# A new hand-written order for the first 36 tiles, with some small steps moved between ScalarE and VectorE

## The chip, the cores and the metric

The kernel runs on one core of a Trainium2 chip. The metric is device time in microseconds, the median of three runs; lower is better.

## The reference

A chunked attention with memory tokens feeds two feed-forward layers, all in fp32. Cut to what matters:

```python
def _attn_ref(q, k, v, mem_k, mem_v):           # 4 x 8 heads, 768 tokens, head size 64
    for c in range(nc):                         # chunks of 32 queries
        k_ctx = k[:, :, l_start:r_end]          # 16 tokens to the left, 8 to the right
        k_full = np.concatenate([mem_k, k_ctx], axis=2)     # 8 memory tokens in front
        scores = scale * np.matmul(q_c, k_full.transpose(0, 1, 3, 2))
        a = np.exp(scores - np.max(scores, axis=-1, keepdims=True))
        a = a / (np.sum(a, axis=-1, keepdims=True) + 1e-09)
        out[:, :, c_start:c_end] = np.matmul(a, v_full)

def _moe_ref(x, w_in, w_out, s, b):             # x 3072 x 512, w_in 512 x 2048
    r = np.maximum(x @ w_in, 0.0)
    return (s * (r * r) + b) @ w_out

def _moe2_ref(x, w_in, w_out):
    h = x @ w_in
    return (h - np.tanh(h)) @ w_out
```

## The kernel before

The 3072 tokens are 24 units of 128 tokens (attention) and 6 blocks of 512 (the layers). A full-precision product is three matmuls on split operands: a rounded upper part and a remainder of both the weights and the data (helper `three`, lines 227 to 229). The order of work of the first 36 up-projection tiles is not found by a scheduler: the string `START` lists it token by token, and each engine runs its own instructions in that order. A token is a step and a number:

- Attention of unit u: `qk` and `vv` load its operands; `S` computes scores on TensorE (line 357); `M` scales and masks them out of PSUM (VectorE, line 380); `R` takes the row maximum (VectorE, line 390); `E` is eight exponentials on ScalarE, each followed by the read-out of its sum (line 398); `D` is a reciprocal and the division (VectorE, lines 412 and 413; a small addition on GpSimd stands before them); `T` transposes on TensorE (line 422 for whole heads, eight instructions, or line 429 for half heads, sixteen); `C` is two copies out of PSUM (ScalarE, line 437); `V` multiplies by the values (TensorE, line 466); `X` and `L` make the upper part (ScalarE, line 484) and the remainder (VectorE, line 488) of the result. Units 0 and 1 come in halves, marked a and b.
- Up-projection weights n = 0 to 7 of the first layer: `ra` loads the words; `z` scales (ScalarE, line 234); `i` shifts (VectorE, line 240); `o` fills (VectorE, line 250); `h` writes the upper part (ScalarE, line 541); `l` the remainder (VectorE, line 545). Tiles 2n and 2n+1 of a block need weights n.
- Tile p: `F` is its 12 products on TensorE (`G` and `F` halves for tiles 0 and 1), into PSUM bank 5 + p mod 3; `r` is the relu (ScalarE, line 572); `Q` the square (ScalarE, line 584, for the tiles in `SCALAR_SQUARES`, else VectorE, line 586). Tile p + 3 can't start before the square of tile p has read that bank.
- `k`, `K`, `st` combine (VectorE, line 598) and store four tiles; `wl`, `ws`, `wf`, `wd`, `wc`, `ww` prepare weights of the second layer (`wc` is four VectorE sums on 128x256, lines 936 and 864; `ww` stores them).

Behind `START` a loop runs tiles 36 to 95, with the same order in both kernels. For tile 36 it says: the products, then the exponentials of unit 16, then the relu of tile 36, then its square:

```python
        up1_products(n)
        ...
            if i8 in (0, 2) and a + i8 // 2 < NU:
                exponentials(a + i8 // 2)
        ...
        up1_relu(n)
        up1_square(n)
```

So on ScalarE the relu of tile 36 stands behind the exponentials of unit 16, and these need `R16`, the last VectorE step of `START`. The tables under `START` (`SCORES_AT`, `TURNS_AT`, `VALUES_BETWEEN`) choose PSUM banks for units; `WHOLE_TURNS` chooses the form of the transposes.

Of the kernel before, what the change touches and what calls it, by code (L numbers as in the profile page):

```python
# [8 lines left out]
F32 = mybir.dt.float32  # L9
# [26 lines left out]


START = """
qka1 Sa1 Ma1 Ra1 Ea1 qkb0 qka0 qkb1 Sb0 Mb0 Rb0 Sa0 Eb0 Ma0 Ra0 Ea0 Sb1 Mb1 Rb1 qk2 Eb1 qk3 S2 M2
qk4 R2 S3 vv0 qk5 S4 vv1 D0 M3 T0 S5 E2 R3 D1 M4 C0 D2 E3 V0 R4 T1 T2 ra0 C1 vv2 X0 D3 M5 V1 T3 vv3  # L40
C2 z0 X1 qk6 L0 i0 C3 h0 V2 L1 V3 S6 o0 l0 G1 ra1 X2 qk7 G0 R5 M6 L2 E4 ra2 vv4 X3 D4 T4 z1 S7 i1
qk9 qk8 L3 h1 E5 o1 F0 l1 z2 r0 C4 F1 R6 i2 F2 h2 E6 Q0 ra3 F3 o2 D5 l2 M7 T5 V4 C5 qk10 D6 r2 R7 S9
z3 r3 S8 i3 ra4 M9 Q2 r1 o3 F5 h3 X4 F4 l3 T6 R9 Q1 z4 E7 L4 M8 vv5 i4 o4 r4 F6 h4 qk11 ra5 Q4 r5 R8
F7 Q5 Q3 z5 l4 C6 r7 F8 S10 vv7 i5 k0 S11 h5 r6 vv9 vv6 V5 o5 E8 Q7 X5 r8 l5 M10 V6 D7 X6 D8 K0 ra6
T7 z6 F11 Q6 E9 F9 qk13 C7 M11 ra7 z7 r9 i6 L6 k1 L5 o6 qk12 h6 R11 F10 i7 h7 D9 T8 S12 r10 l6 C8
st0 vv8 E11 M12 V7 S13 o7 T9 Q8 M13 r11 R13 F12 F13 E13 l7 qk15 X7 R10 Q11 qk14 K1 C9 wl1 F14 S15
vv11 D13 D11 L7 M15 R15 S14 Q9 Q10 ws1 r13 r12 M14 V9 E15 V8 T13 T11 st1 wf1 F15 C11 wc1 qk17 r14
D15 k2 Q12 V11 Q14 S17 r15 X11 L11 wl0 vv13 F18 M17 ww1 F17 R17 E10 Q13 D10 K2 Q15 X9 C13 X8 r17 T10
L9 T15 C10 R14 vv10 V13 L8 V10 k3 C15 r18 K3 F16 r16 R12 F21 X10 st2 E12 F19 Q16 L10 Q18 Q17 r19 r21
F20 F24 Q19 r20 E14 F22 r22 qk16 D12 st3 Q20 F23 r23 Q21 F25 k4 Q22 F26 ws0 Q23 K4 r24 r26 F27 st4  # L50
D14 k5 r25 K5 Q24 F28 Q25 Q26 r27 wd1 F29 st5 Q27 F30 r29 r28 Q29 k6 K6 r30 st6 Q28 F31 F32 X13 Q30
r31 L13 T12 T14 Q31 r32 k7 K7 Q32 F35 r35 F34 Q35 C12 r34 F33 vv12 Q34 wf0 r33 st7 wc0 S16 V12 Q33
k8 K8 wd0 ww0 st8 X12 M16 L12 R16 C14
"""

WEIGHTS2 = {
# [19 lines left out]
for q in (3, 4, 5, 6):  # L76
# [5 lines left out]
PAIRED, UP_FIRST = 16, 36  # L82
QUARTERS = [(j, q) for j in range(2) for q in range(4)]
SCALAR_SQUARES = {
    1, 2, 3, 6, 7, 8, 9, 10, 11, 12, 13, 14, 15, 16, 17, 18, 20, 21, 22, 23, 24, 25, 29, 31, 32, 34,
    35, 39, 47, 89, 90, 91, 92, 93,
}
WHOLE_TURNS = {
    0, 2, 3, 6,
}  # L90
SCORES_AT = {
    0: 5, 1: 2, 2: 0, 3: 5, 4: 0, 5: 5, 6: 0, 7: 2, 8: 0, 9: 2, 10: 0, 11: 2, 12: 0, 13: 2, 14: 0,
    15: 2, 16: 2, 17: 0,
}
TURNS_AT = {
    0: 2, 1: 0, 2: 2, 3: 0, 4: 0, 5: 0, 6: 2, 7: 0, 8: 2, 9: 0, 10: 2, 11: 0, 12: 2, 13: 2, 14: 0,
    15: 0,
}
VALUES_BETWEEN = {
    0, 2, 6, 8, 10, 11,  # L100
}
HIGH_ON_VECTOR = set()
COPY_ON_VECTOR = set()
PLAIN_EXPONENTIALS = set()

P2_STEPS = {}
for m, n, at in ((2, 44, (-2, 1, 2, 6)), (3, 52, (-2, 1, 2, 6)), (4, 60, (-2, 1, 2, 6)), (5, 68, (-2, 1, 2, 6)),
# [34 lines left out]
def tile_chunk_attention_two_ffn(  # L142
# [42 lines left out]
    def new(place, n, dt, name):  # L185
        assert n <= SIZE[place[0]], (place, n)
        if place[0] in "QSRYWV":
            assert place[0] in side["letters"], place
        pool = arena if place[0] in "EZ" else side["of"]
        return pool.tile([P, n], dt, tag=place, name=name)  # L190
# [201 lines left out]
    def exponentials(u, w=None):  # L392
        if u not in sum_t:
            sum_t[u] = small.tile([P, 8], F32, tag="sums", name="sums")
        sm, nmx, sums = sm_t[u], mx_t[u], sum_t[u]
        total = (u, w) not in PLAIN_EXPONENTIALS
        for h in range(8) if w is None else (2 * w, 2 * w + 1, 4 + 2 * w, 5 + 2 * w):
# [1025 lines left out]
```

## Time and profile before

| | |
|---|---|
| median of 3 runs | 1028.63 us (1028.47 to 1029.04) |
| the profiled execution | 1029.12 us, its span 1027.3 us |
| TensorE busy | 1015.4 us, 99% |
| VectorE busy | 788.6 us, 77% |
| ScalarE busy | 573.2 us, 56% |
| granted TensorE clock | 1.00 |

The profile gives start and length of every instruction. Rows of a timeline hold: start and length in us, engine, line, operation, what is written from what, shape, count, and in brackets how long the engine stood idle before and what ended that. Neighbours on an engine overlap a little (one starts before the end of the one in front), so the distance of two starts, not the length, is the price of one in a row. Matmul lengths overlap most: the price of a 128x512 one is the distance of starts.

### The profile page before, as it was taken

How to read it: one execution, taken by the hardware profiler on the slowest of the kernel's cores; microseconds unless marked ns; L12 is line 12 of the kernel's file. 1: busy time of each engine (PE TensorE's matmuls, PEld its weight loads, DVE VectorE, ACT ScalarE, POOL GpSimd, SP SyncE). 2: the span in 40 equal slices, each digit the busy share in tenths (PEclk: the TensorE clock that was granted, in tenths of full speed). 3: DMA queues.
4: the chain of work that ended last, by engine and by line, in shares of the span. 5: the costliest groups of instructions: out<-in, count | busy, mean ns of one | idle time of the engine just before them, and what ended most of it. 6: DMA issues, size and time to landing. Idle time of an engine off the chain costs nothing.

```text
span 1027.3 us, 15607 instructions
## 1 busy us (share of the span) xinstructions
PE 1015.4 (99%) x6112; PEld 842.0 (82%) x6112; DVE 788.6 (77%) x970; ACT 573.2 (56%) x1055; POOL 11.3 (1%) x53
## 2 busy tenths in 40 slices
PE   7999999999999999999999999999999999999998
PEld 5888888888888888888888888888888888888887
DVE  7999446888677878898788788888888966767654
ACT  8999635666435575666555544455445554444432
POOL 1000000000000000000000000000000000000000
PEclk9999999999999999999999999999999999999999
DMA  9798558888889997796652265655569995555761
GB/s 348 295 330 335 243 220 324 327 334 301 325 322 376 387 336 256 259 337 192 209 196 82 113 247 210 238 215 216 226 260 357 364 328 180 200 205 213 256 248 63
DMA packets 78506, 268.94 MB, mean 262 GB/s; under 512 B 5728, under 2 KB 5984, under 8 KB 67168
## 3 DMA queue, kind: packets, MB, share of 16 engines
q1 hardware_dynamic: 78432, 267.94, 70.8%
q8 instruction: 48, 0.79, 0.3%
q14 instruction: 26, 0.21, 0.1%
HBM read 160.96 MB, written 106.95 MB: 261 GB/s over the span
## 4 chain that ended last, share of the span: by engine, by line
PE 93%; DVE 3%; ACT 2%; DMA 1%; issue 0%; SPq 0%; DVEq 0%; ACTq 0%
PE pb L227 30%; PE pb L229 29%; PE pb L228 29%; PE pb L466 2%; PE pb L357 1%; PE pb L429 1%; ACT sm L398 1%; DMA o<-ob 1%; DMA qk<-in_qk_dram 1%; DVE oa L1167 0%; DVE nmx L390 0%; DVE sm L380 0%; DVE oa L864 0%; ACT pt L437 0%; DVE ob L864 0%
## 5 line engine op out<-in xcount | busy, mean ns | idle before, releaser
L228 PE MATMUL pb<-ringhringl,whl 128*128 128x512 f32 (+1 forms) x680 | 262.9, 387 | 0.0
L227 PE MATMUL pb<-ringhringl,whl 128*128 128x512 f32 (+1 forms) x680 | 262.8, 387 | 0.0
L229 PE MATMUL pb<-ringhringl,whl 128*128 128x512 f32 (+1 forms) x680 | 262.8, 386 | 0.0
L738 ACT ACTIVATE ringhringl<-part 128x1024 fp32r<-128x1024 f32 x120 | 127.0, 1060 | 149.0 <-PE pb L229 146.1
L739 DVE TENSOR_TENSOR ringhringl<-part,ringhringl 128x1024 fp32r<-128x1024 f32 x120 | 146.8, 1223 | 73.3 <-ACT ringhringl L738 73.0
L227 PE MATMUL pb<-xh,w 128*128 128x512 f32 (+1 forms) x392 | 152.9, 390 | 0.3 <-DVE oa L586 0.3
L228 PE MATMUL pb<-xh,w 128*128 128x512 f32 (+1 forms) x392 | 151.0, 385 | 0.1
L229 PE MATMUL pb<-xl,w 128*128 128x512 f32 (+1 forms) x392 | 151.0, 385 | 0.0
L229 PEld LDWEIGHTS pb<-ringhringl,whl 128*128 128x128 f32 x680 | 127.7, 188 | 26.1
L228 PEld LDWEIGHTS pb<-ringhringl,whl 128*128 128x128 f32 x680 | 127.7, 188 | 25.9
L227 PEld LDWEIGHTS pb<-ringhringl,whl 128*128 128x128 f32 x680 | 127.7, 188 | 25.7
L572 ACT ACTIVATE r<-pb 128x512 f32<-128x512 f32 x96 | 56.6, 595 | 91.9 <-PE pb L229 90.1
L227 PE MATMUL pb<-x2hx2l,w 128*128 128x512 f32 x224 | 87.3, 390 | 0.2 <-ACT keep L1163 0.2
L227 PEld LDWEIGHTS pb<-xh,w 128*128 128x128 f32 x392 | 73.6, 188 | 16.6 <-DVE oa L586 1.0
L228 PE MATMUL pb<-x2hx2l,w 128*128 128x512 f32 x224 | 87.2, 389 | 0.0
L229 PE MATMUL pb<-x2hx2l,w 128*128 128x512 f32 x224 | 87.1, 389 | 0.0
L229 PEld LDWEIGHTS pb<-xl,w 128*128 128x128 f32 x392 | 73.7, 188 | 15.0
L228 PEld LDWEIGHTS pb<-xh,w 128*128 128x128 f32 x392 | 73.7, 188 | 14.4 <-DVE w L545 0.3
L586 DVE TENSOR_TENSOR oa<-pb,r 128x512 f32<-128x512 f32 x62 | 42.5, 688 | 49.3 <-ACT r L572 49.3
L733 ACT ACTIVATE ringhringl<-part,b_c 128x1024 fp32r<-128x1024 f32 x48 | 55.1, 1151 | 34.1 <-PE pb L229 32.3
L1175 ACT ACTIVATE pb<-oa 128x512 f32<-128x512 f32 x72 | 43.2, 600 | 55.3 <-DVE oa L1167 54.4
L398 ACT ACTIVATE sm<-sm,nmx 128x96 f32<-128x96 f32 x192 | 69.2, 369 | 3.5 <-DVE nmx L390 3.5
(131 smaller groups left out, 1382.0 us busy)
## 6 DMA issues: line engine op xcount, KB each, us to landing
part<-o SPq DMA_DIRECT2D x84, 512.0 KB, 4.9
part<-o SPq DMA_DIRECT2D x42, 1024.0 KB, 6.2
o<-ob SPq DMA_DIRECT2D x24, 1024.0 KB, 5.4
o<-oa SPq DMA_DIRECT2D x24, 1024.0 KB, 3.9
o<-oa SPq DMA_DIRECT2D x24, 768.0 KB, 5.4
o<-ob SPq DMA_DIRECT2D x24, 768.0 KB, 5.1
raw<-in_wi_dram SPq DMA_DIRECT2D x16, 1024.0 KB, 6.4
raw<-in_wo_dram SPq DMA_DIRECT2D x16, 1024.0 KB, 8.2
```

The source lines that it names most:

```text
L227: nc.tensor.matmul(acc, lhsT=whi, rhs=xhi, start=first, stop=False, skip_group_check=more)
L228: nc.tensor.matmul(acc, lhsT=wlo, rhs=xhi, start=False, stop=False, skip_group_check=more)
L229: nc.tensor.matmul(acc, lhsT=whi, rhs=xlo, start=False, stop=last, skip_group_check=more)
L357: nc.tensor.matmul(score_bank(u, g)[QE * e:QE * (e + 1), KE * (r0 + r):KE * (r0 + r + 1)], lhsT=tq[sl, r, QE * e:QE * (e + 1)], rhs=tk[sl, ...
L398: nc.scalar.activation(out=sm[:, h, :], in_=sm[:, h, :], func=AF.Exp, bias=nmx[:, h:h + 1], scale=1.0, **({"accum_out": sums[:, h:h + 1]} ...
L466: nc.tensor.matmul(value_bank(u)[64 * g:64 * g + 64, c0:c0 + QE], lhsT=tv[0:KE, e, 2 * r + g, :], rhs=pt[0:KE, e, 4 * g + r, :], start=Tru ...
L572: nc.scalar.activation(out=r, in_=up_ps[p], func=AF.Relu)
L586: nc.vector.tensor_tensor(out=o, in0=ps2, in1=r2, op=ALU.mult)
L733: nc.scalar.activation(out=xh, in_=src, func=AF.Identity, bias=self.bias)
L738: nc.scalar.activation(out=xh, in_=src, func=AF.Copy)
L739: nc.vector.tensor_tensor(out=xl, in0=src, in1=xh.bitcast(F32), op=ALU.subtract)
L1175: nc.scalar.activation(out=self.rs[o], in_=src, func=AF.Tanh)
```

## The change

`START` is a new list of the same tokens, plus `Ua1`, `U10` and `U14`. Where these stand, the exponentials of that unit (the first half of unit 1; units 10 and 14) run without the read-out of sums, and one VectorE reduction makes the sums. The upper part of weights 1, 2, 3, 4 and 6 is written by VectorE in place of ScalarE, as a multiplication by a per-partition scalar. The two copies of units 12 and 14 go to VectorE. `SCALAR_SQUARES` gains tiles 0, 4, 5, 19, 27, 28, 30 and 33, and loses 20, 22 and 23: 27 of the first 36 squares stood on ScalarE, now 32. Three units are transposed whole (0, 3, 8), before four (0, 2, 3, 6). The bank tables differ too. The code for all of this was there before; its tables were empty.

```diff
-k8 K8 wd0 ww0 st8 X12 M16 L12 R16 C14
...
+k6 r31 K6 Q31 L13 r32 k7 st6 wd0 Q32 K7 F35 F33 F34 r35 C12 ww1 Q35 qk16 r33 Q33 vv12 V12 r34 Q34 k8
+K8 X12 wc0 L12 st7 C14 ww0 S16 M16 R16 st8
 """
...
 WHOLE_TURNS = {
-    0, 2, 3, 6,
+    0, 3, 8,
 }
...
-HIGH_ON_VECTOR = set()
-COPY_ON_VECTOR = set()
-PLAIN_EXPONENTIALS = set()
+HIGH_ON_VECTOR = {
+    1, 2, 3, 4, 6,
+}
+COPY_ON_VECTOR = {
+    12, 14,
+}
+PLAIN_EXPONENTIALS = {
+    (1, 0), (10, None), (14, None),
+}
```

VectorE at the end of the list, before: the last combine (`k8`, `K8`), then `M16`, `L12`, `R16`; behind them stand the squares of tiles 36 and 37.

```order
L586 TENSOR_TENSOR oa<-pb,r 128x2x256
L598 TENSOR_TENSOR ob<-oa 128x512
L598 TENSOR_TENSOR ob<-oa,ob 128x512
L598 TENSOR_TENSOR ob<-oa 128x512
L598 TENSOR_TENSOR ob<-ob,oa 128x512
L380 SCALAR_TENSOR_TENSOR sm<-pb,mask_mid 128x768
L488 TENSOR_TENSOR xl<-pb,xh 128x4x128
L390 TENSOR_REDUCE nmx<-sm 128x8
L586 TENSOR_TENSOR oa<-pb,r 128x2x256 x2
```

The same place now (the lines stand six further down in the file):

```order
L604 TENSOR_TENSOR ob<-ob,oa 128x512
L942 TENSOR_TENSOR raw<-zw 128x256
L870 TENSOR_TENSOR raw<-zw 128x256
L870 TENSOR_TENSOR raw<-raw,zw 128x256
L870 TENSOR_TENSOR raw<-zw,raw 128x256
L494 TENSOR_TENSOR xl<-pb,xh 128x4x128
L441 COPY pt<-pb 96x512 x2
L386 SCALAR_TENSOR_TENSOR sm<-pb,mask_mid 128x768
L396 TENSOR_REDUCE nmx<-sm 128x8
L592 TENSOR_TENSOR oa<-pb,r 128x2x256 x2
```

The four sums of `wc0` and the two copies of `C14` now stand between the last combine and the maximum of unit 16.

ScalarE at the same place, before: the copies of unit 14, the eight exponentials of unit 16, the relus of tiles 36 and 37.

```order
L484 ACTIVATE xh<-pb 128x4x128
L437 ACTIVATE pt<-pb 96x512 x2
L398 ACTIVATE sm,sums<-sm,nmx 128x96 x8
L572 ACTIVATE r<-pb 128x512 x2
L398 ACTIVATE sm,sums<-sm,nmx 128x96 x8
```

And now:

```order
L578 ACTIVATE r<-pb 128x512
L590 ACTIVATE oa<-r 128x2x256
L490 ACTIVATE xh<-pb 128x4x128
L404 ACTIVATE sm,sums<-sm,nmx 128x96 x8
L578 ACTIVATE r<-pb 128x512 x2
```

The copies are gone from ScalarE, and the relus of tiles 36 and 37 still stand behind the exponentials of unit 16.

VectorE around the remainder of weights 7 (the last row that writes `w`), before:

```order
L545 SCALAR_TENSOR_TENSOR w<-raw,root,w 128x1024
L380 SCALAR_TENSOR_TENSOR sm<-pb,mask_first 128x768
L250 SCALAR_TENSOR_TENSOR raw<-raw,z 128x1024
L380 SCALAR_TENSOR_TENSOR sm<-pb,mask_mid 128x768
L390 TENSOR_REDUCE nmx<-sm 128x8
L545 SCALAR_TENSOR_TENSOR w<-raw,root,w 128x1024
```

And now, from the upper part of weights 6 on:

```order
L543 TENSOR_SCALAR w<-z,root 128x1024
L246 TENSOR_SCALAR z<-z 128x1024
L551 SCALAR_TENSOR_TENSOR w<-raw,root,w 128x1024
L386 SCALAR_TENSOR_TENSOR sm<-pb,mask_mid 128x768
L418 RECIPROCAL rs<-sums 128x8
L419 TENSOR_TENSOR sm<-sm,rs 128x768
L396 TENSOR_REDUCE nmx<-sm 128x8
L256 SCALAR_TENSOR_TENSOR raw<-raw,z 128x1024
L604 TENSOR_TENSOR ob<-oa 128x512
L604 TENSOR_TENSOR ob<-oa,ob 128x512
L551 SCALAR_TENSOR_TENSOR w<-raw,root,w 128x1024
```

Ahead of `l7` VectorE now has five upper parts (one is seen here), one reduction of sums, two `D`, one `M` and one `R` more, and three squares fewer.

## Rows read from the trace of the kernel before

**Rows 1.** Windows: stretch and its length, busy us of each engine, clock, DMA.

```profile
0.00:34.00 34.00, 25.87 (x486) 22.16 (x487) 27.54 (x43) 29.68 (x113) 5.20 (x34) 1.00 0.89 339
30.00:100.00 70.00, 69.73 (x928) 58.04 (x929) 65.73 (x88) 67.94 (x213) 3.83 (x9) 1.00 0.87 325
...
170.00:1027.30 857.30, 854.03 (x4341) 708.28 (x4339) 662.90 (x788) 439.77 (x631) 1.39 (x6) 1.00 0.69 254
```

**Rows 2.** Timeline of TensorE from tile 36 to tile 39.

```profile
153.90 0.50 PE L227 MATMUL pb<-xh,w 128*128 128x512 f32 x1
...
161.97 0.39 PE L229 MATMUL pb<-xl,w 128*128 128x512 f32 x1
162.62 0.50 PE L227 MATMUL pb<-xh,w 128*128 128x512 f32 x1 [0.26 <-DVE oa L586]
```

**Rows 3.** Timeline of ScalarE in the same stretch and just behind.

```profile
154.51 1.07 ACT L437 ACTIVATE pt<-pb 96x512 f32<-96x512 f32 x2
158.37 0.38 ACT L398 ACTIVATE sm<-sm,nmx 128x96 f32<-128x96 f32 x1 [2.79 <-DVE nmx L390]
...
161.26 1.05 ACT L572 ACTIVATE r<-pb 128x512 f32<-128x512 f32 x2
...
170.42 1.13 ACT L234 ACTIVATE zq<-raw 128x1024 f32<-128x1024 f32 x1 [1.43 <-DMA raw<-in_wo_dram]
```

**Rows 4.** Timeline of VectorE in the same stretch.

```profile
152.74 0.69 DVE L586 TENSOR_TENSOR oa<-pb,r 128x512 f32<-128x512 f32 x1 [5.62 <-ACT r L572]
153.34 0.68 DVE L598 TENSOR_TENSOR ob<-oa 128x512 f32<-128x512 f32 x1
...
155.87 0.95 DVE L380 SCALAR_TENSOR_TENSOR sm<-pb,mask_mid 128x768 f32<-128x768 f32 x1
156.74 0.68 DVE L488 TENSOR_TENSOR xl<-pb,xh 128x512 fp32r<-128x512 f32 x1
157.34 0.94 DVE L390 TENSOR_REDUCE nmx<-sm 128x8 f32<-128x768 f32 x1
161.87 1.29 DVE L586 TENSOR_TENSOR oa<-pb,r 128x512 f32<-128x512 f32 x2 [3.59 <-ACT r L572]
```

**Rows 5.** Timeline of VectorE: first and last of the four sums of wc0.

```profile
145.56 0.43 DVE L936 TENSOR_TENSOR raw<-zw 128x256 f32<-128x256 f32 x1
...
146.69 0.42 DVE L864 TENSOR_TENSOR raw<-zw,raw 128x256 f32<-128x256 f32 x1
```

**Rows 6.** VectorE groups by shape, 0 to 160 us: count, busy, mean ns, idle.

```profile
L413 DVE TENSOR_TENSOR sm<-sm,rs 128x768 f32<-128x768 f32 x16 | 15.4, 960 | 0.6
...
L488 DVE TENSOR_TENSOR xl<-pb,xh 128x512 fp32r<-128x512 f32 x14 | 9.6, 684 | 3.9 <-ACT xh L484 3.7
...
L240 DVE TENSOR_SCALAR z<-z 128x1024 int32<-128x1024 int32 x8 | 5.5, 690 | 1.7 <-ACT z L234 1.6
L412 DVE RECIPROCAL rs<-sums 128x8 f32<-128x8 f32 x16 | 3.2, 198 | 3.0 <-POOL sums L411 2.9
```

**Rows 7.** Windows: the stretch up to the end of the remainder of weights 7.

```profile
4.80:77.90 73.10, 68.72 (x999) 57.60 (x1000) 69.16 (x94) 71.27 (x241) 4.45 (x12) 1.00 0.89 333
```

**Rows 8.** Timeline of VectorE: the remainder of weights 7.

```profile
76.62 1.28 DVE L545 SCALAR_TENSOR_TENSOR w<-raw,root,w 128x1024 fp32r<-128x1024 f32 x1
```

**Rows 9.** Timeline of TensorE: first product of tile 14; scores of units 15 and 14.

```profile
80.16 0.39 PE L227 MATMUL pb<-xh,w 128*128 128x512 f32 x1
...
82.97 1.55 PE L357 MATMUL pb<-qk 64*64 64x96 f32 x64
```

**Rows 10.** ScalarE groups by shape, 0 to 160 us.

```profile
L584 ACT ACTIVATE oa<-r 128x512 f32<-128x512 f32 x27 | 16.2, 630 | 0.1
L541 ACT ACTIVATE w<-z,root 128x1024 fp32r<-128x1024 f32 x8 | 9.3, 1158 | 1.0 <-DVE z L240 1.0
```

**Rows 11.** Chain of work that ended last: transposes of a unit by halves, and whole.

```profile
39.98 0.58 PE pb L429 x16
...
48.79 0.87 PE pb L422 x8
```

More of the change, by code (lines that the diff above doesn't have):

```diff
@@ L38 @@
 START = """
[L39 to L52, printed above, removed]
-k8 K8 wd0 ww0 st8 X12 M16 L12 R16 C14
+qka0 Sa0 Ma0 Ra0 qkb0 Sb0 Mb0 Ea0 Rb0 qka1 Sa1 qkb1 Ma1 Eb0 qk3 Ra1 Sb1 Mb1 Rb1 ra0 qk2 qk4 S3 qk5
@@ new lines @@
+Ea1 Eb1 D0 vv0 M3 Ua1 R3 T0 S2 z0 D1 S4 M2 C0 i0 E3 M4 R2 vv3 vv1 D3 T1 qk6 qk7 C1 S5 V0 vv2 E2 T3
+V1 ra1 M5 X0 qk8 o0 S6 D2 L0 X1 C3 h0 L1 T2 S7 R4 C2 M6 V3 l0 ra2 V2 R5 M7 X3 z1 X2 L2 G1 E4 i1 L3
+E5 vv5 G0 F0 r0 o1 vv4 h1 F1 l1 R6 ra3 F2 D4 qk9 T4 z2 D5 r1 T5 vv6 E6 i2 C4 R7 C5 h2 r2 o2 vv8 F3
+D6 z3 S9 Q1 qk10 S8 Q0 l2 M9 ra4 V5 M8 V4 vv10 X5 i3 E7 X4 h3 S10 z4 r3 L5 R9 T6 F4 r4 o3 M10 F5 l3
+R8 i4 qk11 C6 F6 qk12 Q4 E9 D7 Q3 ra5 Q2 h4 T7 o4 S11 D9 vv7 L4 F7 qk13 qk14 C7 M11 z5 T9 i5 r6 V7
@@ new lines @@
+E8 k0 r5 l4 o5 V6 S13 vv9 C9 r7 R11 M13 h5 Q5 R13 S12 F8 ra6 X6 E13 Q7 l5 z6 D8 F10 K0 qk15 r8 Q6 T8
+L6 D13 F9 C8 i6 M12 S15 S14 ra7 z7 o6 h6 st0 E11 i7 r10 l6 vv11 h7 M15 X7 r9 D11 F11 R15 o7 E15 wl1
+Q8 k1 l7 F13 r11 F12 Q9 Q11 ws1 D15 r12 qk17 R10 K1 wf1 F14 F15 r14 wc1 M14 L7 V9 T11 Q10 E10 T13 X9
+L9 U10 V8 D10 C11 V11 r13 X8 X11 S17 C13 L11 M17 st1 Q12 F16 R17 r15 T10 T15 Q13 L8 vv13 V13 k2 r16
+C10 C15 V10 Q15 F17 K2 X10 Q14 R12 L10 F18 E12 r17 R14 st2 F20 F19 k3 K3 r18 E14 Q17 Q16 r19 r20 Q18
@@ L54 @@
+st3 Q19 D12 F21 F22 k4 K4 Q20 r21 r22 wl0 ws0 Q22 F24 F23 F25 st4 U14 Q21 r23 r25 Q23 F26 k5 r26 Q26
+r24 Q24 F28 Q25 K5 wd1 st5 F27 r27 Q27 r28 F29 F30 F31 wf0 r29 D14 r30 Q29 F32 Q30 T12 T14 Q28 X13
+k6 r31 K6 Q31 L13 r32 k7 st6 wd0 Q32 K7 F35 F33 F34 r35 C12 ww1 Q35 qk16 r33 Q33 vv12 V12 r34 Q34 k8
+K8 X12 wc0 L12 st7 C14 ww0 S16 M16 R16 st8
 """
@@ L84 @@
 SCALAR_SQUARES = {
-    1, 2, 3, 6, 7, 8, 9, 10, 11, 12, 13, 14, 15, 16, 17, 18, 20, 21, 22, 23, 24, 25, 29, 31, 32, 34,
-    35, 39, 47, 89, 90, 91, 92, 93,
+    0, 1, 2, 3, 4, 5, 6, 7, 8, 9, 10, 11, 12, 13, 14, 15, 16, 17, 18, 19, 21, 24, 25, 27, 28, 29,
+    30, 31, 32, 33, 34, 35, 39, 47, 89, 90, 91, 92, 93,
 }
 WHOLE_TURNS = {
-    0, 2, 3, 6,
+    0, 3, 8,
 }
 SCORES_AT = {
-    0: 5, 1: 2, 2: 0, 3: 5, 4: 0, 5: 5, 6: 0, 7: 2, 8: 0, 9: 2, 10: 0, 11: 2, 12: 0, 13: 2, 14: 0,
-    15: 2, 16: 2, 17: 0,
+    0: 5, 1: 0, 2: 2, 3: 5, 4: 5, 5: 0, 6: 5, 7: 2, 8: 0, 9: 2, 10: 2, 11: 2, 12: 2, 13: 0, 14: 0,
+    15: 2, 16: 0, 17: 2,
 }
 TURNS_AT = {
-    0: 2, 1: 0, 2: 2, 3: 0, 4: 0, 5: 0, 6: 2, 7: 0, 8: 2, 9: 0, 10: 2, 11: 0, 12: 2, 13: 2, 14: 0,
+    0: 0, 1: 2, 2: 0, 3: 2, 4: 2, 5: 0, 6: 0, 7: 0, 8: 0, 9: 2, 10: 2, 11: 2, 12: 0, 13: 0, 14: 2,
     15: 0,
@@ L99 @@
 VALUES_BETWEEN = {
-    0, 2, 6, 8, 10, 11,
+    1, 2, 5, 6, 9, 10, 11,
 }
-HIGH_ON_VECTOR = set()
-COPY_ON_VECTOR = set()
-PLAIN_EXPONENTIALS = set()
+HIGH_ON_VECTOR = {
[7 more added lines that the diff above has]
+}
 P2_STEPS = {}
```

## The prediction

> **What bounds the kernel now.** I read the windows first. TensorE is 99% busy over the span and its granted clock is 1.00 throughout, so there is no clock to win. Behind 170 us it is busy 854.03 of 857.30 us [rows 1]: there a change of order among the first 36 tiles has nothing to fill, and whatever TensorE loses or gains ahead of that point stays in the total. From 30 to 100 us it idles only 0.27 us (70.00 less 69.73) [rows 1]. Real idle time lies in the first 34 us (25.87 busy, 8.1 idle) [rows 1], and one more wait stands at tile 39: its first product starts at 162.62 and waited for a square on VectorE [rows 2]. From 153.90 to 161.97 there are 35 distances of one matmul, 8.07 / 35 = 0.23 us each, so TensorE alone would have been there at 162.20; the wait is worth 0.42 us [rows 2].
>
> Then I read who sets these two places. Early on it is VectorE with ScalarE: up to the end of the remainder of weights 7 VectorE is busy 69.16 of 73.10 us and ScalarE 71.27 [rows 7]. At the end of the list it is one chain. On VectorE the last square starts at 152.74, the combine at 153.34, `M16` at 155.87, `L12` at 156.74 and `R16` at 157.34, ending at 158.28 [rows 4]. The exponentials of unit 16 follow on ScalarE at 158.37, the relus of tiles 36 and 37 at 161.26 [rows 3], the square of tile 36 on VectorE at 161.87 [rows 4], and tile 39, which needs that square's bank, at 162.62 [rows 2]. From the end of `R16` to tile 39 it is 4.34 us, and the loop that follows holds this order in both kernels.
>
> **The change part by part.** *End of the list.* From the start of the combine to the end of `R16` it is now 158.28 - 153.34 = 4.94 us [rows 4]. The new list puts two things into this stretch. The four sums of `wc0` took 145.56 to 147.11 [rows 5], 1.55 alone and about 1.47 in a row, since neighbours overlap by some 0.08 (the square of 0.69 is followed after 0.60 [rows 4]). They stood in a gap before: VectorE idled 5.62 us ahead of the last square [rows 4]. The two copies of `C14` took 1.07 on ScalarE [rows 3]; no row shows a copy of this kind on VectorE. The nearest rows are two operations of 512 that read PSUM there, 1.29 together [rows 4], or 0.684 each [rows 6]: in a row about 1.2. The other bound is the in-SBUF operation of 1024 elements with one tensor input, 0.690 [rows 6], which would make it 0.7. I take 1.2, because the operand lies in PSUM. `R16` also stands right behind `M16`, whose result it reads, where `L12` stood between: 0.1. Sum 1.47 + 1.2 + 0.1 = 2.8, with 2.3 and 3.0 as ends. The chain starts with the last product of the last tile of the group in both lists, the same two score and value steps and three tiles stand behind it on TensorE, and behind `R16` nothing changes. So tile 39 starts 2.8 later against TensorE's own work, which waits about 0.42 + 2.8 = 3.2 us there. Queued behind `R16` are the exponentials, and behind them the relu and square of tile 36: nothing can take the loss up, as TensorE runs its tiles in order and has no spare products ahead of tile 39. ScalarE, relieved of the copies, only waits longer.
>
> *Head.* What VectorE must do ahead of the remainder `l7` sets when tile 14 may start. Against before, the list has there two `D` more (0.960 + 0.198 each [rows 6], 2.32), one `M` and one `R` more (0.95 and 0.94 [rows 4]), the sums of half a unit (half of an `R`, 0.5), five upper parts, and three squares fewer (0.69 each, 2.07 [rows 4]). An upper part on VectorE is in no row. Its bounds are 0.690, an operation with one tensor of 1024 [rows 6], and 1.28, the remainder, which reads two [rows 8]; I take 0.69, the row with as many tensors, so 3.45. Sum 2.32 + 1.89 + 0.5 + 3.45 - 2.07 = 6.1, less 0.08 overlap for nine more instructions, 5.4. `l7` ended at 77.90 [rows 8]; it ends at 83.3 if VectorE idles as before (3.9 us [rows 7]) and at 79.4 if all that idle time is filled. ScalarE is relieved by 5 x 1.158 less five more squares at 0.630 [rows 10] and the read-outs, some 3 us, which should fill a part of it: I take 81.5.
>
> TensorE reached tile 14 at 80.16, and behind it came the scores of units 15 and 14, 1.47 us without the overlap [rows 9]. The new list has both ahead of tile 14, and one of the whole-unit transposes (0.87) becomes one by halves (0.58 [rows 11]). So TensorE comes to tile 14 at 80.16 + 1.47 - 0.29 = 81.35. A wait of 0 to 2 us for `l7` follows. I take 0.6, less the 0.29 that TensorE saves for good: +0.3, with -1.0 (the relieved ScalarE also shortens some of the 8.1 us of idle time ahead of 34 us) and +2.0 as ends.
>
> At double duration of the upper parts the head costs 5 x 0.59 = 2.95 more VectorE work. The Trainium skill bears on this price. The row shows 0.690 for 1024 elements from one tensor in SBUF and 0.684 for 512 out of PSUM [rows 6]. "VectorE: DVE Perf Modes", section "Mode 2×_2P — use both read ports for one tensor", says that a single-source fp32 operation within SBUF uses both read ports and gets two elements per cycle, and that PSUM has one port, so that nothing read from there does. By it the five upper parts stay at 3.45, and the two copies at 1.2; by the other ends they would be 6.4 and 0.7, and the sum 2.4 higher. The trace agrees for the rows named; no run so far shows an upper part or a copy on VectorE.
>
> *The rest.* Between 85 and 150 us the sums of units 10 and 14 and the copies of unit 12 come to VectorE; what hides them is its slack (it idled 5.62 us ahead of the last square alone [rows 4]). Without that cover they would cost up to 0.94 or 1.2 each. `ww0`, the store of the sums, now waits for the later `wc0` and stands ahead of `st8` and the first load of the last matrix on SP's queue. Those words landed at 170.42 and are then scaled for 1.13 on ScalarE [rows 3]; about 3 us later, the scaling stands ahead of another relu, whose bank TensorE needs two tiles on, over 5 us later. Nothing; if that slack were gone, 1.1. The sum is +0.3 + 2.8 = **+3.1**. The profiled execution took 1029.12 us, 0.49 above the median of 1028.63: 1032.2 on its basis, 1031.7 on the median's.
>
> **The rivals.** *A, VectorE is later at tile 14.* An upper part costs 1.28, or VectorE idles as before in spite of the relief: `l7` ends at 83.3 to 86, tile 14 waits 2 to 4.6 us. For it: upper part and remainder of one set now share an engine. Against it: [rows 6] for one tensor. Head +1.7 to +4.3, total +4.5 to +7.1: 1033.1 to 1035.7.
>
> *B, the head gains more than the end loses (the other side).* VectorE and ScalarE are both full ahead of 78 us [rows 7], and moving work between them and changing the order of the loads may let dense work on TensorE begin earlier. It decides if tile 14 starts 5 us ahead of its arrival worked out above, so before 76.3; then 2.8 - 5.2 = -2.4, 1026.2. For it: 8.1 us of idle time ahead of 34 us [rows 1]. Against it: `l7` ends no earlier than 79.4 with 5.4 us more work ahead of it, so tile 14 can't start so early.
>
> *C, the two cancel.* The copies cost 0.7 (end +2.3) and the head gains 1.0 to 2.5: -0.2 to +1.3, 1028.4 to 1029.9. For it: the filled idle time. Against it: the same bound on `l7`.
>
> *D, the change doesn't do what it says.* The lists of both engines show the moved instructions at the places told above; what is left is that the last steps are not on the path, since tile 39 waits for something else. The 0.26 us on that square speaks against it [rows 2]; C's time would follow.
>
> **How the numbers follow.** The forecast, +1.5 to +4.5, has 0.62; A 0.16; B 0.07; C with D 0.15. I count as no change what lies within 0.2%, 2.06 us, about what a measurement of this kernel can tell from none. Faster is B, 0.07. Same are C and D, 0.15, and the low part of the forecast up to 1030.7, 0.05: 0.20. Slower is the rest, 0.73. The range takes the forecast's ends (2.3 - 1.0 = +1.3 below; 3.0 + 2.0 = +5.0 above), the upper half of C and the most of A: 1029.2 to 1034.6, which leaves out B, the lower part of C and the upper third of A, 2 in 10.
>
> **What would show it.** Right: TensorE waits about 3.2 us at tile 39 for a VectorE square; between combine and `R16` stand the sums at 1.5 and two copies at about 0.6 each; the end of `R16` to tile 39 is 4.3 again. `l7` ends at 81.5 and tile 14 starts within 1 us of it or without a wait; an upper part takes 0.69. Before 34 us TensorE idles about 8 us as now. Wrong: tile 14 starting before 79 us or after 84; a wait at tile 39 under 2 us, which would mean that the sums or the copies hide; or a new wait of over 0.5 us anywhere from 85 to 150 us.

## The result

| | before | after |
|---|---|---|
| median of 6 runs | 1028.56 us | 1037.74 us |
| lowest and highest run | 1028.39, 1029.51 | 1034.90, 1039.27 |
| the profiled execution, its span | 1029.12, 1027.3 us | 1037.81, 1036.0 us |

The change makes the kernel slower by 9.2 us by the medians; the ratio of the means is 1.0084, with a 95% interval of 1.0069 to 1.0099. The forecast was 1031.7, with 1034.6 as the upper end: the sign and one mechanism were forecast, the size was not. The runs of after also lie 4.4 us apart, those of before 1.1.

Windows of after (columns as in [rows 1], with which they compare):

```profile
0.00:34.00 34.00, 24.07 (x475) 20.80 (x476) 26.79 (x43) 28.00 (x103) 5.36 (x34) 1.00 0.88 329
30.00:100.00 70.00, 66.59 (x847) 54.56 (x846) 65.12 (x88) 64.37 (x213) 5.36 (x10) 1.00 0.81 294
100.00:160.00 60.00, 60.00 (x429) 49.54 (x428) 29.55 (x46) 31.23 (x71) 0.90 (x2) 1.00 0.64 245
```

TensorE idles 9.93 us ahead of 34 us (8.13 before) and 3.41 us from 30 to 100 us (0.27 before): about 4.9 us more, in two stretches that overlap by 4 us. From 100 to 160 us nothing is lost.

Timeline of TensorE in after, the end of tile 38 and tile 39 (compare [rows 2]), and two windows around it:

```profile
166.67 0.39 PE L235 MATMUL pb<-xl,w 128*128 128x512 f32 x1
170.16 0.72 PE L233 MATMUL pb<-xh,w 128*128 128x512 f32 x1 [3.10 <-DVE oa L592]
170.68 0.63 PE L234 MATMUL pb<-xh,w 128*128 128x512 f32 x1
171.10 0.63 PE L235 MATMUL pb<-xl,w 128*128 128x512 f32 x1
...
173.66 0.41 PE L235 MATMUL pb<-xl,w 128*128 128x512 f32 x1
173.91 0.40 PE L233 MATMUL pb<-xh,w 128*128 128x512 f32 x1
```

```profile
165.00:170.16 5.16, 2.06 (x11) 1.37 (x9) 1.58 (x3) 4.24 (x21) 0.23 (x1) 1.00 1.00 343
...
171.00:172.00 1.00, 1.00 (x4) 0.71 (x4) 0.80 (x1) 1.00 (x7) 0.00 (x0) 0.50 1.02 415
```

Tile 39 starts at 170.16, 7.54 us later than before. The distance of two starts just behind is 0.43 us in place of 0.23, since the granted clock is 0.50, the lower of its two levels (1.2 in place of 2.4 GHz). The first nine distances take 3.75 us; before they took 0.34 + 8 x 0.23 = 2.2. That is 1.6 us more. 7.5 + 1.6 is a little above the difference of the spans, 8.7: some 0.4 us come back later. Of these 0.2 us are a wait for ScalarE that before has later on and after has not; the rest I did not trace. Not every run of after shows the lower clock: its mean over the run is 0.994 to 0.998 in five of the six and 1.000 in one, which took 1036.15 us.

Timeline of VectorE at the same place (compare [rows 4]):

```profile
158.10 0.69 DVE L604 TENSOR_TENSOR ob<-oa 128x512 f32<-128x512 f32 x1 [8.53 <-ACT oa L590]
...
160.63 0.42 DVE L942 TENSOR_TENSOR raw<-zw 128x256 f32<-128x256 f32 x1
...
162.10 0.68 DVE L494 TENSOR_TENSOR xl<-pb,xh 128x512 fp32r<-128x512 f32 x1
162.70 1.27 DVE L441 COPY pt<-pb 96x512 f32<-96x512 f32 x2
163.90 0.94 DVE L386 SCALAR_TENSOR_TENSOR sm<-pb,mask_mid 128x768 f32<-128x768 f32 x1
164.88 0.95 DVE L396 TENSOR_REDUCE nmx<-sm 128x8 f32<-128x768 f32 x1
```

An upper part on VectorE, which no row of before showed:

```profile
75.64 0.75 DVE L543 TENSOR_SCALAR w<-z,root 128x1024 fp32r<-128x1024 f32 x1
```

From the combine to the end of `R16` it is 165.83 - 158.10 = 7.73 us (4.94 before): the sums take 1.47, the copies 1.20. From there to tile 39 it is 4.33. This term came out as worked out, 2.79.

### The profile page after: what moved, and what is told of

Same layout as the page of the kernel before. It is cut to its first block, busy times and chain, and to the rows that moved or that the text cites. A ratio compares the mean times of both kernels' runs of the same rounds, so it can differ in the third digit from the quotient of the medians.

```text
span 1036.0 us, 15609 instructions
## 1 busy us (share of the span) xinstructions
PE 1016.7 (98%) x6120; PEld 842.6 (81%) x6120; DVE 793.0 (77%) x977; ACT 568.7 (55%) x1031; POOL 13.1 (1%) x53
## 4 chain that ended last, share of the span: by engine, by line
PE 91%; ACT 3%; issue 2%; DVE 2%; DMA 1%; SPq 0%; POOL 0%; ACTq 0%; POOLq 0%
PE pb L233 29%; PE pb L234 29%; PE pb L235 29%; ACT sm L404 2%; PE pb L472 1%; DMA raw<-in_wi_dram 1%; PE pb L363 1%; PE pb L435 1%; DMA qk<-in_qkh_dram 0%; ACT r L578 0%; DVE sm L386 0%; DVE nmx L396 0%; DVE ob L604 0%; DVE raw L256 0%; ACT oa L590 0%
## 5 line engine op out<-in xcount | busy, mean ns | idle before, releaser
L740 DVE SCALAR_TENSOR_TENSOR ringhringl<-part,b_c,ringhringl 128x1024 fp32r<-128x1024 f32 x48 | 61.5, 1282 | 12.9 <-ACT ringhringl L739 12.8
```

What stands on the lines that cost most here:

```text
L740: nc.vector.scalar_tensor_tensor(out=xl, in0=src, scalar=self.bias, in1=xh.bitcast(F32), op0=ALU.add, op1=ALU.subtract)
```

## Experiments at the end of the list

Theory: the wait at tile 39 comes from what stands ahead of `R16`, and the fall of the clock from that wait. `t1_r16_first` puts `M16` and `R16` back ahead of the sums and copies, with `S16` one step earlier on TensorE. The sums, and so their store `ww0`, then stand behind `R16`:

```diff
-... V12 r34 Q34 k8 K8 X12 wc0 L12 st7 C14 ww0 S16 M16 R16 st8
+... S16 V12 r34 Q34 k8 K8 X12 M16 L12 R16 wc0 st7 C14 ww0 st8
```

> The changed kernel with M16 and R16 back ahead of the sums wc0 and of the copies of unit 14 at the end of the list (S16 one step earlier on TensorE). Theory: the 3.5 us at tile 39 come from what stands between the combine and R16, and the fall of the granted clock to 0.50 behind it comes from that idle time. Then the wait falls to 0.3 to 0.8 us, the clock stays 1.00 behind 165 us, and the time falls by 2.8 + 1.2 = 4.0 us, to about 1033.7. Rival 1: the fall of the clock has another cause; then it stays and the gain is 2.8, to 1034.9. Rival 2: the loss ahead of 150 us reaches tile 39 in another way; gain below 1 us.

Measured: 1038.06 us, ratio to before 1.0094 (1.0067 to 1.012): no gain, though its four runs lie 7.2 us apart. The wait at tile 39 did go to 0.32 us. Timelines of this kernel, some 15 to 20 us behind tile 39: ScalarE, then TensorE, and a window on TensorE's clock:

```profile
181.87 1.16 ACT L240 ACTIVATE zq<-raw 128x1024 f32<-128x1024 f32 x1 [7.87 <-DMA raw<-in_wo_dram]
182.93 1.55 ACT L578 ACTIVATE r<-pb 128x512 f32<-128x512 f32 x3
```

```profile
186.27 1.15 PE L472 MATMUL pb<-pt,v 96*64 96x64 f32 x32 [2.18 <-DVE oa L592]
187.73 0.65 PE L435 MATMUL pb<-ident,sm 64*96 64x64 f32 x16 [0.31 <-DVE sm L386]
```

```profile
189.48:192.00 2.52, 2.52 (x8) 2.04 (x7) 2.52 (x4) 2.40 (x10) 0.00 (x0) 0.50 1.03 419
```

A second wall stood behind the first. ScalarE waits 7.87 us for the first words of the last matrix, three relus queue behind their scaling, then the squares, and TensorE waits 2.18 us and more; the clock falls again. The reason is on SP's queue. SP's issue of these words in before; the store `ww0` and the issue of the words in after; the issue of the words here:

```profile
159.52 0.50 SPq L519 DMA_DIRECT2D raw<-in_wo_dram  x1
```

```profile
162.21 0.32 SPq L948 DMA_DIRECT2D w2z<-raw  x1
...
168.45 0.56 SPq L525 DMA_DIRECT2D raw<-in_wo_dram  x1
```

```profile
171.31 0.49 SPq L525 DMA_DIRECT2D raw<-in_wo_dram  x1
```

The store `ww0` (first row of after) waits for the sums `wc0`, and behind it on SP stand the stores `st8`, four loads of units, and these words. They land 10 to 11 us after their issue: scaled at 170.42 before [rows 3], at 181.87 here. ScalarE's scaling of these words in after:

```profile
178.81 1.12 ACT L240 ACTIVATE zq<-raw 128x1024 f32<-128x1024 f32 x1 [0.67 <-DMA raw<-in_wo_dram]
```

That is 8.4 us later than before, of which 4.7 are the lateness with which TensorE came to the end of the list; 3.7 are left for the store. In after TensorE has no wait behind tile 39, so there the late store cost nothing. t1 itself makes the words 3.1 us later still, as it puts the sums behind `R16`, and that stops TensorE. So this run shows where the slack ends; it doesn't give the price of the store in after.

`t2_sums_behind` moves only the sums behind `R16`:

```diff
-k8 K8 X12 wc0 L12 st7 C14 ww0 S16 M16 R16 st8
+k8 K8 X12 L12 st7 C14 S16 M16 R16 wc0 ww0 st8
```

> The changed kernel with only the four sums wc0 moved behind R16; the two copies on VectorE stay ahead of it. The wait at tile 39 falls by 1.5 to about 2.0 us. Theory: an idle time of 2 us is too short for the clock to fall, so the time falls by 1.5 + 1.2 = 2.7 us, to 1035.0. Rival: the clock falls after 2 us as after 3.5 us; then the gain is 1.5, to 1036.2.

Measured: 1039.06 us, 1.0107 (1.0082 to 1.0131). On time it missed for the same reason: the sums and the store are behind `R16` here too, the words are scaled at 181.94 and TensorE waits again at 186 us. On the clock it tells: TensorE's wait at tile 39, and the window behind it:

```profile
168.19 0.50 PE L233 MATMUL pb<-xh,w 128*128 128x512 f32 x1 [1.63 <-DVE oa L592]
```

```profile
168.19:171.00 2.81, 2.81 (x12) 2.31 (x13) 1.62 (x3) 2.81 (x16) 0.08 (x1) 1.00 1.03 408
```

After 1.63 us of idle time the clock stayed 1.00; after 3.10 it had fallen.

`b2_late_r16` does the harm alone, in the kernel before:

```diff
-... st7 wc0 S16 V12 Q33 k8 K8 wd0 ww0 st8 X12 M16 L12 R16 C14
+... st7 S16 V12 Q33 k8 K8 X12 wc0 L12 C14 M16 R16 wd0 ww0 st8
-COPY_ON_VECTOR = set()
+COPY_ON_VECTOR = {14}
```

> The kernel before with wc0 and the copies of unit 14 (now on VectorE) put between the combine and M16, R16, as in the changed kernel; all else as before. Theory: tile 39 starts 2.8 us later and the clock falls behind it as in the changed kernel: +2.8 + 1.2 = 4.0 us, 1032.6. Rival: the fall of the clock belongs to the head of the new list; +2.8, 1031.4.

Measured: 1033.70 us, 1.0055 (1.0038 to 1.0071), 5.2 us above before by the medians. The span of its profiled run, the lowest of four, is 4.0 us longer (1031.3 against 1027.3). All four have a mean clock of 0.997 or 0.998. Tile 39 and the window behind it:

```profile
164.87 0.50 PE L227 MATMUL pb<-xh,w 128*128 128x512 f32 x1 [3.03 <-DVE oa L586]
```

```profile
164.87:168.00 3.13, 3.13 (x10) 2.57 (x11) 1.66 (x4) 3.05 (x16) 0.23 (x1) 0.74 1.03 414
```

So the end of the list makes the wait and the fall of the clock by itself, without the new head. The store is late here too, and the words are scaled 3.4 us later than before:

```profile
173.79 1.12 ACT L234 ACTIVATE zq<-raw 128x1024 f32<-128x1024 f32 x1 [0.95 <-DMA raw<-in_wo_dram]
```

TensorE has no wait behind tile 39, so this lateness costs nothing either.

`t4_ww0_only` moves the sums and their store into the gap of VectorE ahead of the last combine, and leaves the copies ahead of `R16`; `t3_ww0_early` restores the whole end.

```diff
-... r33 Q33 vv12 V12 r34 Q34 k8 K8 X12 wc0 L12 st7 C14 ww0 S16 M16 R16 st8
+... r33 Q33 st7 wc0 ww0 vv12 V12 r34 Q34 k8 K8 X12 L12 C14 S16 M16 R16 st8      (t4)
+... r33 Q33 st7 wc0 ww0 vv12 S16 V12 r34 Q34 k8 K8 st8 X12 M16 L12 R16 C14      (t3)
```

> The changed kernel with only the sums wc0 and their store moved to the gap of VectorE ahead of the last combine; the two copies of unit 14 stay on VectorE ahead of M16 and R16. Theory of two walls: the wait at tile 39 falls by the 1.5 us of the sums to about 1.7 to 2.0 us, too short for the clock to fall; the words of the last matrix are scaled by 177 us, and no wait follows at 186 us. Time: 1.5 + 1.2 = 2.7 us below the changed kernel, 1035.0, and above t3 by the rest of the wait, 1.3 to 2. Rival: the store alone was the second wall and R16 costs nothing then; time as t3, 1032.9.

> The changed kernel with the whole end of its list as before: the sums wc0 and their store ww0 ahead of the last combine, M16 and R16 right behind it, the copies of unit 14 (on VectorE) last; everything ahead of tile 33 as in the changed kernel. Theory: two walls stand one behind the other. R16 behind the sums and copies stops TensorE at tile 39; and the store ww0, which waits for the sums, holds up SP's queue, so that the first words of the last matrix land late (181.9 us with R16 alone moved), which stops TensorE at 186 us. With both gone the waits at tile 39 and at 186 us are below 0.5 us, the words are scaled by 176 us, the clock stays 1.00 and the time falls by about 4 us to 1033.7; 1029.3 + 4.7 of the head is 1033.3. Rival: a further wait behind these two takes the gain back; then it stays above 1036.

Measured: t4 1033.74 us, 1.0042 (1.0026 to 1.0059), 1.3 us below its forecast, with the scaling at 173.14 and a mean clock of 1.000 in all four runs. Tile 39 of t4:

```profile
166.84 0.50 PE L233 MATMUL pb<-xh,w 128*128 128x512 f32 x1 [1.25 <-DVE oa L592]
```

t3 1032.89 us, 1.0039 (1.0028 to 1.005). TensorE's waits of t3 from 36 us to the end (columns: who waited for whom, us in total, times, longest):

```profile
PE pb L233 <- ACT r L578: 0.8, 2, 0.4
PE pb L363 <- DMA qk<-in_qk_dram: 0.5, 1, 0.5
PE pb L233 <- DVE oa L592: 0.3, 1, 0.3
```

The end of the list costs 1037.74 - 1032.89 = 4.9 us. By the medians, `R16` put ahead of the sums gives back nothing (t1), the sums with their store put early give back 4.0 (t4), the whole end 4.9 (t3). t4's early sums also take 1.5 us out of `R16`'s way, and behind the 1.25 us of wait that are left the clock stays. t3 lies 4.2 us above the kernel before that ran beside it and t4 4.5, so the times don't tell these two apart: that `R16` costs nothing once the sums are early is not excluded by them, only t4's wait of 1.25 us against t3's 0.3 speaks against it.

`b3_r16_first` puts `M16 R16` of the kernel before even ahead of its last combine (`Q33 M16 R16 k8 K8 wd0 ww0 st8 X12 L12 C14`).

> The kernel before with M16 and R16 ahead of the last combine, L12 behind it. Theory: the 0.42 us lost at tile 39 go, as the exponentials of unit 16 then end about 1.8 us earlier; the store st8 and the first words of the last matrix come 1.8 us later, to 172.2, which is hidden. Time 1028.1, 0.4 lower, or the same within the measurement. Rival: the later words stop TensorE at 180 to 186 us, +1 us or more.

Measured: 1028.49 us, 0.9996 (0.9987 to 1.0006): the same. The wait at tile 39 is gone and the profiled span is 0.7 us shorter, but the times don't tell the two apart. No kernel that I ran beats the one before.

## Experiments ahead of 100 us

Of the 9.2 us, 4.2 remain in t3 (1032.89 us, with 1028.74 for before beside it). In t3's trace TensorE has only 0.3 us of wait behind the last score and value steps, so the loss arises ahead of them. TensorE's first of these in before, in after, and in t3:

```profile
152.00 0.89 PE L357 MATMUL pb<-qk 64*64 64x96 f32 x32
```

```profile
156.70 1.15 PE L472 MATMUL pb<-pt,v 96*64 96x64 f32 x32
```

```profile
154.56 0.89 PE L363 MATMUL pb<-qk 64*64 64x96 f32 x32
```

Up to there after and t1 to t4 give TensorE the same steps in the same order. Yet it comes there at 156.70 in after, 156.94 in t1, 156.20 in t2, 154.56 in t3 (the fastest run of its eight) and 155.23 in t4: the head costs 2.6 to 4.9 us, and differs from run to run. VectorE's window up to the end of the remainder of weights 7 in after, and that remainder (compare [rows 7, 8]):

```profile
4.80:86.30 81.50, 72.73 (x1080) 60.14 (x1080) 74.46 (x102) 73.95 (x265) 6.36 (x15) 1.00 0.90 331
```

```profile
85.02 1.28 DVE L551 SCALAR_TENSOR_TENSOR w<-raw,root,w 128x1024 fp32r<-128x1024 f32 x1
```

VectorE has 74.46 - 69.16 = 5.3 us more work, as counted (5.4). But its idle time grew from 3.9 to 7.0 us and ScalarE's from 1.8 to 7.6, while `l7` ends at 86.30. Both engines stand waiting, for each other and for loads. What TensorE waits for from 36 to 100 us in after:

```profile
PE pb L363 <- ACT r L578: 0.9, 1, 0.9
PE pb L233 <- ACT r L578: 0.9, 2, 0.5
PE pb L363 <- ACT pt L443: 0.8, 1, 0.8
PE pb L363 <- DMA qk<-in_qk_dram: 0.4, 1, 0.4
```

It is never VectorE. (A square on ScalarE reads the relu's result and not the PSUM bank, so for the tiles in `SCALAR_SQUARES` it is the relu, not the square, that frees the bank.) Timelines of ScalarE and TensorE at the second row:

```profile
76.19 1.18 ACT L240 ACTIVATE z<-raw 128x1024 f32<-128x1024 f32 x1 [1.67 <-DMA raw<-in_wi_dram]
...
80.14 0.57 ACT L578 ACTIVATE r<-pb 128x512 f32<-128x512 f32 x1
```

```profile
80.77 0.50 PE L233 MATMUL pb<-xh,w 128*128 128x512 f32 x1 [0.47 <-ACT r L578]
...
86.92 0.50 PE L233 MATMUL pb<-xh,w 128*128 128x512 f32 x1 [0.41 <-ACT r L578]
```

ScalarE waits 1.67 us for the words of weights 7, runs eight exponentials from 77.27 on, and only then the relu that tile 13 needs. At 86.92 it is tile 14, and again a relu. `l7`, the remainder that the prediction had tile 14 wait for, had ended 0.6 us earlier, at 86.30.

`b1_upper_on_vector` is the kernel before with `HIGH_ON_VECTOR = {1, 2, 3, 4, 6}` alone.

> The kernel before, its list untouched, with the upper parts of weights 1, 2, 3, 4 and 6 on VectorE. Theory A: the 3 us lost between 34 and 100 us come from this move, since each remainder ends later and the next load of words, which needs its buffer, starts later; then +1.5 to +3 us, with waits of TensorE between 34 and 100 us. Rival B: they come from the new order (exponentials of a unit queued ahead of a relu on ScalarE, a remainder queued behind a step that waits for a load); then this kernel is within 0.5 us of before.

Measured: 1030.36 us, 1.0015 (1.0006 to 1.0025). In the old order the move costs 1.8 us. That is the time of Theory A, but not its way: all eight loads of words are issued within 0.8 us of before's, and TensorE's longest wait behind 34 us is for a square on VectorE:

```profile
53.12 0.50 PE L229 MATMUL pb<-xh,w 128*128 128x512 f32 x1 [1.00 <-DVE oa L588]
```

`h1_upper_on_scalar` is the reverse, t3 with `HIGH_ON_VECTOR = set()`.

> The kernel t3 (end of the list repaired) with the five upper parts back on ScalarE. Theory A: the 4.7 us that TensorE has lost by tile 36 come for 1.8 us from the upper parts on VectorE, as the kernel before showed with that part alone; then the time falls by 1 to 2 us below t3. Rival B: in the new order ScalarE is what TensorE waits for (relus queued behind exponentials), and 5 x 1.1 us more on it costs 1 to 3 us.

Measured: 1038.24 us, 1.0102 (1.0072 to 1.0131), 5.3 us above t3, so B, and more than it said. TensorE's waits there from 34 us on:

```profile
PE pb L231 <- ACT r L576: 3.4, 2, 3.0
PE pb L231 <- ACT w L545: 1.8, 1, 1.8
PE pb L232 <- DVE w L549: 0.8, 1, 0.8
```

The new order can't do without the move: ScalarE is what TensorE mostly waits for there. `h3_all_upper` adds weights 5 and 7 to t3's set, `h2_relus_first` moves four relus, a square and a remainder:

```diff
-C7 M11 z5 T9 i5 r6 V7 E8 k0 r5 l4 o5 ... ra7 z7 o6 h6 st0 E11 i7 r10 l6 ... R15 o7 E15 wl1 Q8 k1 l7 F13 r11
+C7 M11 r5 r6 l4 z5 T9 i5 V7 E8 k0 o5 ... ra7 r10 z7 o6 h6 st0 E11 i7 l6 ... R15 o7 Q8 r11 E15 wl1 k1 l7 F13
```

> The kernel t3 with the relus of tiles 5, 6, 10 and 11 ahead of the exponentials or the scaling they stood behind on ScalarE, and the remainder of weights 4 ahead of the shift of weights 5, which waits for a load. Theory B: this order costs the waits of TensorE at 65 us (0.82), 81 us (0.47) and 87 us (0.41): the time falls by 1.2 to 1.8 us below t3. Rival A (VectorE's total of work and the loads set the pace): these waits only move, gain below 0.5 us.

> The kernel t3 with the upper parts of weights 5 and 7 on VectorE as well. Putting five of them back on ScalarE cost 5.3 us, so ScalarE's queue is what TensorE waits for between 34 and 92 us. If that holds for these two, whose relus and scalings follow them closely, 0.5 to 1.5 us below t3. If VectorE is by now as tight (remainder 7 ends at 86.3, and 1.3 us more work stand ahead of it), 0.5 to 1.5 us above.

Measured: h2 1032.66 us, 1.0036 (1.0024 to 1.0048), as t3. The waits of tiles 13 and 14 went, but one of 0.7 us for VectorE appeared at 94 us, and TensorE idles 1.34 us from 34 to 100 us where t3 idles 1.36: they moved. h3 1034.50 us, 1.005 (1.0033 to 1.0066): no gain either. Two edits in the first 20 us of t3, `S2` ahead of `T0` (`k1_scores_first`) and `(1, 0)` taken out of `PLAIN_EXPONENTIALS` (`k2_sums_on_scalar`):

> The kernel t3 (end of the list repaired) with the scores of unit 2 ahead of the transposes of unit 0 on TensorE, into the 2.4 us for which TensorE stands before these transposes at 12.9 us. If that gap is worth something by itself, TensorE comes 0.8 us earlier to tile 2 and the time falls by 0.5 to 0.8 us below t3. If ScalarE and VectorE set the pace of the first 34 us, nothing changes (within 0.3 us).

> The kernel t3 with the sums of the first half of unit 1 read out on ScalarE again instead of one VectorE reduction (0.54 us at 13.5 us, ahead of the maximum of unit 3, for whose exponentials ScalarE waits). If VectorE's chain sets the pace of the first 20 us, 0.3 to 0.5 us below t3; if ScalarE, up to 0.4 us above it.

Measured: 1033.49 us, 1.0041 (1.0026 to 1.0056), and 1033.76 us, 1.0045 (1.003 to 1.006): neither brings a gain that shows; the 0.3 to 0.8 us at stake are less than the spread of t3's runs, 3.6 us.

To tell stretches apart, three kernels join the two lists: a list up to a product, then the other list's remaining steps in its order, each with its own tables.

```diff
+x1: old list up to F2 (34 us), then the order of t3
+x2: new list up to F2, then the order of before
+x3: old list up to F14 (83 us), then the order of t3
```

> The old list up to the products of tile 2 (34 us), behind it the remaining steps in the order of the new list with its repaired end; the upper parts of weights 2, 3, 4 and 6 on VectorE, the tables of the old list for what it holds. If the loss of the repaired new list (1032.9 against 1028.7) arises ahead of 34 us (profile: 1.4 us there, and all waits for instruction words and falls of the clock seen so far ahead of 100 us), this kernel is near 1029.5 to 1030.5; if it arises from 34 to 92 us (1.7 us in the profile: loads of units and relus behind exponentials), near 1031 to 1032.5.

> The new list up to the products of tile 2, behind it the remaining steps in the order of the old list, with its end and its tables; only the upper part of weights 1 on VectorE. The other half of the same question: 1030.5 to 1032 if the loss arises ahead of 34 us, 1029 to 1030 if behind it.

> The old list up to the products of tile 14 (83 us), behind it the remaining steps in the order of the new list with its repaired end (sums of units 10 and 14 by VectorE, copies of units 12 and 14 on VectorE, squares of the new list). The profile shows no loss from 100 to 160 us, so this should be within 0.3 us of the kernel before, 1028.5 to 1029; if the later part of the new list costs something that only its own lateness hides, 1 us or more above.

Measured: x1 1033.74 us, 1.0045 (1.003 to 1.006); x2 1030.98 us, 1.0024 (1.0014 to 1.0033); x3 1038.74 us, 1.0094 (1.0077 to 1.0111). Windows from 34 to 100 us of x1 and of x2:

```profile
34.00:100.00 66.00, 62.89 (x818) 51.05 (x818) 60.71 (x82) 59.92 (x188) 4.70 (x9) 1.00 0.80 292
```

```profile
34.00:100.00 66.00, 65.54 (x831) 53.63 (x830) 61.13 (x82) 62.76 (x198) 4.04 (x9) 1.00 0.87 308
```

With the old head the new middle still idles 3.1 us on TensorE (x1); with the new head the old middle idles 0.5 us (x2), and x2 is 2.2 us above before. So the new head costs about 2 us. The new order from 34 to 92 us costs about as much: of x1's 3.1 us, 1.2 are a wait at its seam (at 38.59 us, for a division on VectorE), which leaves 1.9. x1 as a whole is 5.0 us above before; its profiled run also has a clock of 0.92 and 0.85 from 10 to 26 us, in the old head. 2.2 and 5.0 don't add up to t3's 4.2, perhaps since a late head gives the middle's loads and relus time, which was not shown. x3 doesn't answer its question: at its seam TensorE waits 7.5 us for a relu. Only the stretch from 100 to 160 us, busy throughout, could be read from it. Which steps within the head and the middle start the loss stays open: none of the single edits brought a gain that shows.

One thing that differs from run to run is a stop in the head. Timeline of TensorE in h2's profiled run (1034.41 us, the highest of its six), and the window behind:

```profile
26.88 1.23 PE L363 MATMUL pb<-qk 64*64 64x96 f32 x21 [1.70 <-issue]
```

```profile
26.00:33.00 7.00, 6.12 (x91) 5.79 (x92) 4.36 (x6) 3.25 (x9) 0.00 (x0) 0.52 0.55 193
```

In the middle of a unit's scores TensorE stands 1.70 us though nothing that the profile shows is missing, and the clock falls for 7 us. t3's profiled run (1031.23) and after's have neither; t1's has such a stop of 1.49 us at the same place, with the clock at 1.00. What TensorE stands for there no trace shows: "waits for instruction words", in the expectation of x1, is a guess.

The mean granted clock is on record for every run. Of t3's eight runs the five at 1.000 took 1031.23 to 1033.11 us, the three at 0.997 or 0.998 took 1034.12 to 1034.85: there the longer runs are those in which the clock fell. It doesn't explain the spread of after, whose only run at 1.000 took 1036.15 and whose lowest, 1034.90, had 0.998.

## Why the prediction was wrong

**What held.** The sign; the stretch from the combine to `R16` (2.79 measured, 2.8 forecast); the wait at tile 39 (166.67 + 0.23 to 170.16 is 3.26, forecast 3.2); the 4.34 behind `R16` (4.33); VectorE's added work ahead of `l7` (5.3, forecast 5.4). Two copies on VectorE took 1.27 and one upper part 0.75, so the prices chosen for them were near. The rule of the Trainium skill, "VectorE: DVE Perf Modes", "Mode 2×_2P — use both read ports for one tensor", agrees: 1024 elements within SBUF in little more time than 512 out of PSUM. Rival A's price of 1.28 was wrong, though a head as late as A's came about in another way. The wait at tile 14 was 0.41 where 0.6 was forecast, but that was luck: `l7` ended 4.8 us later than forecast (86.30 in place of 81.5), and TensorE was done with the tile in front 5.0 us later (at 86.35, 86.12 + 0.23, in place of 81.35). Tile 14 started at 86.92, behind the 84 that the prediction had named as a sign of being wrong.

**Step 1, "there is no clock to win".** I read the clock of 1.00 as a term that could not move, and gave it no sentence. It could fall: behind 3.1 us of idle time it did, for 1.6 us more (after, b2). In these profiled runs the term of the end was 2.8 + 1.6.

**Step 2, the head, "+0.3 with -1.0 and +2.0 as ends".** This is the step that put the time outside the range. TensorE came to the last score and value steps at 156.70 in place of 152.00, +4.7 us, and +2.6 to +4.9 in the other runs with the same steps; even the least of these is above the upper end. I took one gate, `l7` on VectorE against tile 14, let TensorE reach that gate without a loss on the way, and took the engine that was relieved of work as one that can't hold anyone up. The sentence that the relieved ScalarE "should fill a part" of VectorE's idle time is the one that failed: VectorE's idle time rose from 3.9 to 7.0 us, ScalarE's from 1.8 to 7.6.

"Some 3 us" of relief was also counted wrongly. Ahead of `h7`, which `l7` needs, the new list has five upper parts fewer on ScalarE, but three squares, the copies of units 8 and 9 and the exponentials of units 11 and 13 more. By rows (5 x 1.16 less; 3 x 0.63, 4 x 0.5 and 2 x 2.87 more, the last from 77.27 to 80.14 in after) that is an estimated 3.8 us more work there, not 3 less. I had costed the work that was moved between engines, but not the order of the steps between which it was moved, which was all new.

What the runs show in its place: the new head costs about 2 us (x2), the new order from 34 to 92 us about as much (x1), and TensorE's waits in after from 36 to 100 us are for ScalarE, in 2.6 of 3.0 us. That a relu behind eight exponentials makes the loss is not shown: h2 moved four relus ahead and the time stayed. Which steps make it stays open.

**Step 3, the store `ww0`, "Nothing; if that slack were gone, 1.1".** In after this term came out as forecast: there is no wait behind tile 39. The words came 8.4 us later than before and not 3, but 4.7 of that is the late head, and 3.7 are left for the store. What was mis-sized is the price without slack: in t1 and t2, where the words come another 3 us later, TensorE waits 2.18 and 1.65 us at 186 us, more than 1.1, and in t1 the clock falls behind it. I had priced the scaling alone, and not the relus, squares and the next attention steps that queue behind it.

**Step 4, the range.** It took its ends from the terms, and the sum with what was measured is 4.7 + 2.8 + 1.6 = 9.1 in place of 3.1. The runs of after alone lie 4.4 us apart.

## What to carry to other kernels

When a list of steps is rewritten, count the moved work, but also ask, of each engine that feeds the bottleneck, what now stands ahead of the step that the bottleneck waits for; an engine that gave work away can still be the late one. A store that waits for a late result holds up the loads behind it on its queue. A repair can also push something else over its slack, as t1 did with the store: look for the next wait before judging the repair. A clock that stands at full speed in the profile is a price still to be paid once a new wait is long.

## What the runs showed of the hardware

The granted clock of TensorE fell to 0.50 behind idle times of 3.10 us (after) and 3.03 us (b2), and stayed at 1.00 behind 1.63 us (t2, tile 39) and 1.25 us (t4). In b2 it fell only 1.5 us after TensorE had begun again. The length of one stop doesn't settle it: among the small matmuls of the head it fell behind 1.70 us (h2) and stayed behind 1.49 us (t1), and in t1 it fell behind stops of 2.18, 0.31 and 0.21 us with short operations between. At 0.50 the distance of two matmuls is 0.43 us in place of 0.23. And the same order of instructions gave runs 3.6 us apart (t3, 1031.23 to 1034.85), where 13 runs of the kernel before beside other kernels lie 2.4 us apart (1028.19 to 1030.58).
